# A bilinear feed-forward kernel behind memory attention: batch 0's output with plain weights, and all engines in the order of four written lists

## The chip, the cores and the metric

The kernel runs on one core of a Trainium2 chip. The metric is the device time of one launch in microseconds (us); less is better. The core has a matrix engine (TensorE; PE in the profile, its weight loads PEld), a vector engine (VectorE; DVE), a scalar engine (ScalarE; ACT), GpSimd (POOL) and a sync engine (SyncE; SP) that issues all of this kernel's DMAs. In this kernel each engine works through its own list of instructions and waits on semaphores for the others. TensorE's results land in PSUM banks, and ACT and DVE copy them out to the main on-chip memory, SBUF, where POOL's steps work too.

## The reference

There are 8 batches of 8 heads, 576 tokens, head size 64, and 32 memory slots:

```python
a   = softmax(phi, axis=slots)                      # tokens x 32
k_m = einsum('bhsm,bhsd->bhmd', a, k); v_m = einsum('bhsm,bhsd->bhmd', a, v)
x   = softmax(q @ k_m.T / 8) @ v_m                  # attention over 32 memories
out = ((x @ w1) * (x @ w2)) @ w3 @ w_out            # 512 -> 1024, 1024 -> 1024 -> 512
```

The weights arrive as 64-bit floats and the attention inputs as 32-bit floats.

## The kernel before

**The algebra.** The value memories are multiplied into w1 and w2 once per batch (the "M" steps, four per batch, line 316), so that per token only the attention weights over 32 memories per head remain to be multiplied: the "A" units (line 505), 16 per batch, make 128 rows of (x·w1) and (x·w2) for half a batch (288 tokens) each; ACT copies one of the two out of PSUM (`a_sb`, line 513) and DVE multiplies the other with it into `g` (line 515). W = w3·w_out is computed once, at the start, in sixteen product steps (W00 to W07 for its upper half of rows, W10 to W17 for the lower; line 411). The output of a batch is W's transpose times g.

**Precision.** Every product of the A and out units is made of three: an operand is split into a rounded high part (ACT) and the low rest (DVE or POOL), and high·high, low·high and high·low are summed in PSUM. So each operand that is used there costs an ACT step and a subtraction: `mh`/`ml` for M, `ah`/`al` for the attention weights, `sh`/`sl` for g (steps h and l, lines 541 and 547), `Wh`/`Wl` for W.

**Strassen.** The out product of a batch is a 2 x 2 block product (two halves of the tokens by two halves of the output rows) and is made with seven block products instead of eight, in the Winograd form: sums of g's blocks (POOL, lines 520 to 532) times sums of W's blocks. Each of the seven takes two "O" units of 12 matmuls (line 567), 14 per batch. Banks are named o, x and ab; `keep` copies intermediate results out (p1, u2, p5, p4), `result` adds and stores them (C11, C12, C21, C22; line 583). W's blocks need the same sums: `weights_of_out` (line 430) makes, with ACT, DVE and POOL, W0 (upper rows, with the right half replaced by a difference), W1 (lower rows as they are), W2 and W3 (further differences), each with a high and a low part. In the kernel before this is done during batch 0's A units, by the tokens K, T, V, D, E, F, G.

**Conversion.** Each of 22 weight blocks is loaded (line 362) and turned from 64 to 32 bits by `convert` (from line 364): a DVE step (line 390), two ACT steps (391, 393), two DVE steps (399, 400). Five load buffers are in flight; the last blocks are loaded into the attention's own tiles.

**Attention of a batch**, as a chain of named steps: top (DVE) exp (ACT) norm (DVE) turn0, turn4 (TensorE transposes, copied out by ACT) mem (TensorE, copied out by ACT) blocks (TensorE, copied out by DVE), then for each half n of the tokens sc (TensorE scores, transposed out by DVE) mx sb (DVE) ex (ACT) sm mu tr (DVE) ah (ACT) al (DVE).

**Order.** SP and TensorE follow the order in which the code emits. START (line 21) is the order up to the first A unit; in it ACT, DVE and POOL are ordered by the scheduler of the framework. From batch 0 on those three also follow the order of the code: FIRST (line 26) for batch 0's A units, with the last four conversions and the steps on W between them; BATCH_A (line 30) for the A units of the other batches; BATCH_O (line 31) for the out units of all batches. The next batch's attention (STREAM, line 35) is fitted in between by `ahead_slot` (line 597), which goes by a table of costs (line 40) and a limit of load, and which starts only at slot 13, that is, late in batch 0's A units. A tile's buffers are reused when all who read it are done.

Of the kernel before, what the change touches and what calls it, by code (L numbers as in the profile page):

```python
# [19 lines left out]

START = """
C C W00 C phi0 C top W01 C C C W02 kv0 C q0 W03 W04 exp norm C turn0 C W05 C W06 turn4 W07 C K1 mem K0 blocks W10
C W11 K3 K2 sc0 W12 C mx0 sb0 ex0 C sc1 mx1 sb1 ex1 C W13 W14 sm0 mu0 N C sm1 mu1 W15 C W16 W17 tr0 ah0 al0 N
tr1 ah1 al1
""".split()
# [13 lines left out]

COLUMNS = {"A": 439, "h": 0, "l": 727, "C11": 727, "C22": 727, "C21": 727, "C12": 727, "top": 1300, "norm": 330, "blocks": 1110,  # L40
           "sc": 876, "mx": 726, "sb": 726, "sm": 1100, "mu": 726, "tr": 726, "al": 726, "M": 1174, "N": 1174, "C1": 726,
           "C3": 1820, "D": 407, "E": 1060}
TENSOR = {"A": 1517, "O": 1517, "M": 910, "N": 910, "mem": 2300, "turn0": 770, "sc0": 500, "sc1": 500, "blocks": 200}
LIMIT = 2100


def groups(text):
    return [x.split() for x in text.split("|")]


def columns(what):
    return COLUMNS.get(what, COLUMNS.get(what.rstrip("0123456789"), 0))


@with_exitstack
def memory_attention__then__bilinear_ffn_kernel(
# [64 lines left out]
    def split(hi, lo, src):  # L121
        nc.scalar.copy(out=hi, in_=src)  # L122
        nc.vector.tensor_tensor(out=lo, in0=src, in1=hi.bitcast(F32), op=ALU.subtract)  # L123


# [36 lines left out]
    def attention(b):  # L162
# [22 lines left out]
        def turn(i, bank):  # L185
            ps = bank().rearrange("p k (c t x) -> p (k c) t x", c=2, t=NT)
            if i == 0:
                for c in range(4):
                    for t in range(NT):
                        at = t * D + c * P  # L190
                        nc.tensor.transpose(ps[:, c, t], v["ph"][:, t, at : at + P], ident)
                nc.scalar.copy(out=v["a"][:, :4], in_=ps)
            else:
                last = v["ph"].rearrange("p t s -> p (t s)")[:, 4 * P : 5 * P]
                nc.tensor.transpose(ps[:, 0, 0], last, ident)
                nc.scalar.copy(out=v["a"][:, 4, 0], in_=ps[:, 0, 0])

        def memories(bank):
            kvt = loaded.pop(("kv", b))
            v["kvm"] = att.tile([P, NT, 2 * D], F32, name="kvm")  # L200
            ps = bank()
# [10 lines left out]
            for h in range(4):  # L212
                for t in range(NT):
# [22 lines left out]
        def scores(n, bank):  # L236
# [6 lines left out]
            ps = [both[:, t, :HALF] for t in range(NT)]  # L243
# [9 lines left out]
            nb = NBLK // 2  # L253
# [479 lines left out]
```

## Time and profile before

| | |
|---|---|
| median of 3 runs | 568.89 us (568.81 to 569.41) |
| the profiled execution | 569.46 us, span 567.7 us |
| mean granted TensorE clock | 0.986 |
| busy share of the span: TensorE, DVE, ACT, POOL | 94%, 64%, 49%, 25% |
| DMA | 64.13 MB, 113 GB/s over the span |
| first matmul; first A unit | 9.07 us; 74.70 us |
| first A unit of batch 1, of batch 2 | 153.28 us; 216.46 us |
| last matmul begins | 562.30 us |

The profile is one execution, taken by the hardware profiler. A view of groups shows, for a line, engine and operation, how many instructions there were, their busy time, the mean of one in ns, and behind the bar the idle time of the engine just before them with the engine and line that ended it. A view of waits lists who waited for whom: us in total, times, longest. A timeline row has start, duration, engine, line, operation, and in square brackets the idle time before it. The times of matmuls overlap: their durations are modelled, and the distance between the starts of two is what one costs.

### The profile page before, as it was taken

The numbers are of one execution on the slowest core, as the hardware profiler recorded it, in microseconds if no ns is written. First come the engines' busy times: TensorE is split into PE (matmuls) and PEld (weight loads), VectorE is DVE, ScalarE is ACT, GpSimd is POOL, SyncE is SP. The second block draws the span as 40 slices with busy tenths as digits, with TensorE's granted clock in tenths as the row PEclk, the third lists the DMA queues.
The fourth block names the chain that finished last, engine by engine and source line by source line (L and its number), as shares of the span: only waits on it lengthen the run. The fifth ranks groups of instructions, "written<-read, shape, count | busy, mean of one in ns | idle before, by whom it ended". The sixth has DMA issues, their size and how long they took to land.

```text
span 567.7 us, 10851 instructions
## 1 busy us (share of the span) xinstructions
PE 532.0 (94%) x4504; PEld 448.6 (79%) x4504; DVE 365.9 (64%) x598; ACT 276.5 (49%) x465; POOL 141.2 (25%) x154
## 2 busy tenths in 40 slices
PE   3999996869889999999999999999999999999996
PEld 1454475757788899879988898889897998799996
DVE  4857957666744596548753885488448844695463
ACT  6867455564235443545254534453455435453351
POOL 0000016592011520233022502160207010611180
PEclk9999998979999999999999999999999999999999
DMA  8999530705410533043204311342114310001001
GB/s 321 408 382 388 199 97 21 249 0 190 147 42 2 170 105 104 2 169 105 69 36 168 105 64 43 119 133 84 43 51 149 116 64 2 1 26 60 1 22 63
DMA packets 28304, 64.13 MB, mean 113 GB/s; under 512 B 1632, under 2 KB 9824, under 8 KB 28256
## 3 DMA queue, kind: packets, MB, share of 16 engines
q1 hardware_dynamic: 28256, 63.45, 31.6%
q8 instruction: 35, 0.57, 0.4%
q14 instruction: 13, 0.11, 0.1%
HBM read 54.00 MB, written 9.44 MB: 112 GB/s over the span
## 4 chain that ended last, share of the span: by engine, by line
PE 78%; DVE 9%; ACT 7%; DMA 2%; POOL 1%; issue 1%; DVEq 0%; ACTq 0%
PE ab L505 29%; PE x L567 13%; PE o L567 11%; PE ab L567 4%; PE ab L411 4%; PE ab L316 4%; DVE ml L123 3%; ACT mh L122 3%; PE o L316 3%; PE o L411 3%; PE x L411 2%; PE x L205 2%; DVE mx L169 2%; ACT ph L175 2%; DMA raw<-in_w_out 1%
## 5 line engine op out<-in xcount | busy, mean ns | idle before, releaser
L505 PE MATMUL ab<-ah,mh 128*128 128x288 f32 x512 | 155.9, 305 | 8.4 <-DVE g L515 5.5
L505 PE MATMUL ab<-al,mh 128*128 128x288 f32 x512 | 152.7, 298 | 2.0 <-DVE al L292 2.0
L505 PE MATMUL ab<-ah,ml 128*128 128x288 f32 x512 | 151.6, 296 | 0.0
L515 DVE TENSOR_TENSOR g<-ab,a_sb 128x288 f32<-128x288 f32 x128 | 58.2, 455 | 112.0 <-ACT a_sb L513 112.0
L505 PEld LDWEIGHTS ab<-ah,mh 128*128 128x128 f32 x512 | 96.8, 189 | 26.2 <-DVE g L515 19.8
L513 ACT COPY a_sb<-ab 128x288 f32<-128x288 f32 x128 | 50.9, 398 | 124.1 <-PE ab L505 121.8
L547 DVE TENSOR_TENSOR sl<-g,sh 128x576 fp32r<-128x576 f32 x112 | 93.0, 842 | 16.2 <-ACT sh L541 16.1
L505 PEld LDWEIGHTS ab<-al,mh 128*128 128x128 f32 x512 | 96.9, 189 | 3.7 <-DVE al L292 3.7
L505 PEld LDWEIGHTS ab<-ah,ml 128*128 128x128 f32 x512 | 97.2, 190 | 0.0
L520 POOL TENSOR_TENSOR g<-g,g 128x288 f32<-128x288 f32 x32 | 30.7, 958 | 245.0 <-DVE g L515 245.0
L541 ACT CAST sh<-g 128x576 fp32r<-128x576 f32 x112 | 74.9, 675 | 33.8 <-PE x L567 11.9
L567 PE MATMUL o<-sh,Wh 128*128 128x288 f32 x192 | 58.4, 304 | 0.0
L567 PE MATMUL x<-sh,Wh 128*128 128x288 f32 x192 | 57.4, 299 | 0.0
L567 PE MATMUL o<-sh,Wl 128*128 128x288 f32 x192 | 57.2, 298 | 0.0
L567 PE MATMUL o<-sl,Wh 128*128 128x288 f32 x192 | 57.2, 298 | 0.0
L567 PE MATMUL x<-sh,Wl 128*128 128x288 f32 x192 | 56.6, 295 | 0.0
L567 PE MATMUL x<-sl,Wh 128*128 128x288 f32 x192 | 56.6, 295 | 0.0
L528 POOL TENSOR_TENSOR g<-g,g 128x288 f32<-128x288 f32 x32 | 26.0, 835 | 115.7 <-DVE sl L547 115.7
L567 PEld LDWEIGHTS x<-sh,Wh 128*128 128x128 f32 x192 | 36.2, 189 | 5.7 <-issue 5.7
L567 PEld LDWEIGHTS o<-sh,Wh 128*128 128x128 f32 x192 | 36.7, 191 | 3.3 <-issue 3.3
L411 PE MATMUL ab<-wo,w 128*128 128x512 f32 x64 | 29.7, 620 | 9.6 <-DVE wo L400 9.6
L567 PEld LDWEIGHTS o<-sh,Wl 128*128 128x128 f32 x192 | 36.7, 191 | 0.0
(125 smaller groups left out, 875.4 us busy)
## 6 DMA issues: line engine op xcount, KB each, us to landing
kv<-in_kv SPq DMA_DIRECT2D x16, 1024.0 KB, 7.3
q<-in_qT SPq DMA_DIRECT2D x8, 1152.0 KB, 5.5
outT<-c SPq DMA_DIRECT2D x32, 288.0 KB, 2.3
raw<-in_w3T SPq DMA_DIRECT2D x7, 1024.0 KB, 11.9
ph<-in_phiT SPq DMA_DIRECT2D x8, 576.0 KB, 3.9
raw<-in_w SPq DMA_DIRECT2D x4, 1024.0 KB, 17.6
raw<-in_w_out SPq DMA_DIRECT2D x3, 1024.0 KB, 10.0
kv<-in_w SPq DMA_DIRECT2D x3, 1024.0 KB, 14.4
```

The source lines that it names most:

```text
L122: nc.scalar.copy(out=hi, in_=src)
L123: nc.vector.tensor_tensor(out=lo, in0=src, in1=hi.bitcast(F32), op=ALU.subtract)
L316: nc.tensor.matmul(ps[g * M : (g + 1) * M, t], lhsT=vm[b % 2][d, g], rhs=w12_sb[q][d, :, g], start=True, stop=True,)
L411: nc.tensor.matmul(pw[r][i], lhsT=x[:, i * P : (i + 1) * P], rhs=wos[k // half][:, k % half], start=k == 0, stop=k == NF - 1,)
L505: nc.tensor.matmul(both[:, w, :HALF], lhsT=x[:, t, w, fc : fc + P], rhs=y[:, n, t * HALF : (t + 1) * HALF], start=i == 0, stop=i == len(to ...
L513: nc.scalar.copy(out=a_sb, in_=both[:, 0, :HALF])
L515: nc.vector.tensor_tensor(out=G[n, f // half][:, k], in0=both[:, 1, :HALF], in1=a_sb, op=ALU.mult)
L520: gp(out=low, in0=top, in1=low, op=ALU.subtract)
L528: gp(out=s2, in0=s2, in1=s3, op=ALU.subtract)
L541: nc.scalar.copy(out=hi, in_=src)
L547: nc.vector.tensor_tensor(out=lo, in0=src, in1=hi.bitcast(F32), op=ALU.subtract)
L567: nc.tensor.matmul(ps[:, j, :HALF], lhsT=x[s][:, 2 * part + k, jc], rhs=y[:, k], start=i in (1, 4, 2, 5) and part == 0 and k == 0 and t == ...
```

## The change

1. **Batch 0's out is made plainly**: four blocks of g against W's own blocks, 16 units "Q" (`plain_unit`) in place of 14 Strassen units, and four plain copies to the output (d0 to d3, `plain_result`). W's sums for Strassen are made in another order, and their high and low parts partly in batch 1's A units (tokens r, s, w, y, t, z), from copies in the `sh`/`sl` buffers (tokens a and b with a digit).
2. **Each step is on one engine.** Steps that held a TensorE part and a copy are cut in two (turn and turnc, mem and memc, block and blockc, sc and scc, M into M, Mh and Ml); an A unit becomes a generator of three steps (A: TensorE, a: ACT, g: DVE), a conversion one of five (C1 to C5); the sums on POOL become tokens of their own (f0 to f3, S1 to S4).
3. **The order of all engines, from the first instruction, is that of four lists**: START, FIRST (batch 0), SECOND (batch 1) and BATCH (batches 2 to 7). The table of costs, `ahead_slot` and `batches`' rules go. A token with "-" belongs to the batch's own attention, which is now finished inside its own A units; other attention tokens belong to the next batch. A token of an A unit or a conversion advances the next unit or conversion in turn by one step, whichever step that is.
4. `ah` and `al` have one buffer instead of two, and START holds one M step instead of two. Batch 1's A units run in the order (2 x 6 rows, then 2 x 2) instead of (2 x 4, 2 x 2, 2 x 2).

```diff
-START = """ C C W00 C phi0 C top W01 C C C W02 kv0 C q0 W03 W04 exp norm C turn0 ...
+START = """
+C1 C2 C2 C3 C3 C4 C5 C1 C2 C1 C4 C5 C3 C4 W00 phi0 C3 C4 C5 C2 C1 C1 C2 C5 W01 C4 q0 C3 C2 C3 C5 C4 C1 C5 C2 C3 C4 C1
+C3 C2 C1 W02 W03 C5 C4 kv0 top C5 C2 C4 exp norm C2 C1 C1 C3 C3 C5 W04 turn0 turnc0 C4 C5 W05 W06 C1 C4 turn4 C2 C3 C3
+C2 C5 C1 turnc4 W07 K1 Kt1 K0 C4 Kh1 Kt0 Kh0 K2 Kl1 mem K3 Kh3 Kl0 memc block Kh2 Kl3 C2 Kt2 C5 C1 C3 blockc C4 C5 W10
+Kl2 C2 C1 C3 C4 Kt3 sc0 C3 C5 sc1 C2 C1 W11 W12 scc0 C3 W13 C2 C4 mx0 C5 C1 sb0 C4 ex0 C1 sm0 scc1 W14 C5 C4 C2 C3 C2
+C1 M0 mx1 C3 C4 sb1 W15 W16 Mh0 C5 mu0 ex1 sm1 tr0 ah0 C5 Ml0 mu1 al0 tr1 W17 ah1 al1
+"""
 FIRST = """
+phi A a g A C1 M1 C2 C2 a g Mh1 Ml1 C3 C4 A A a g C1 a C5 g C4 C3 A A C5 a g C2 C1 a g M2 Mh2 C3 A a C4 Ml2 C1 g A C2
+a C5 C4 A a g D0 A C3 g C5 A a g q h0 l0 kv Dt0 a g E0 M3 Mh3 Ml3 D1 Et0 F0 D3 A a Dt1 g D2 E1 A A Dt2 a g Et1 F1 E2 A
+a g h1 l1 A a h3 g a g Et2 h2 l2 Dt3 Q E3 Q Q Et3 top h4 l3 Q l4 Q exp norm h5 Q l5 h6 turn0 l6 turn4 turnc4 Q turnc0
+mem memc Q h7 l7 d0 Q kv block F3 d1 Q F2 blockc M0 b1 a0 sc0 scc0 mx0 Mh0 sb0 ex0 Ml0 Q Q Q M1 a2 sc1 Q sm0 mu0 Mh1
+scc1 q a3 b0 tr0 ah0 Q Q d2 al0 a1 d3 Ml1
 """
+SECOND = """
+M2 Mh2 -mx1 r1 -sb1 A a -ex1 g r0 s0 A A a Ml2 r2 g -sm1 A w1 a g a -mu1 -tr1 g w3 -ah1 s1 w0 -al1 phi A a s2 y0 g A A
+r3 M3 a a s3 h1 g g y3 w2 y2 top A t0 y1 t1 a Mh3 t2 g z1 A z0 A f0 a a g g A f1 a Ml3 g exp A A a a g g f3 l1 norm
+turn0 h0 l0 f2 turnc0 t3 A a turn4 g h2 l2 turnc4 S2 A mem memc A z2 a g O a g h3 z3 h4 l3 S3 S1 l4 block O h5 O
+blockc M0 kv l5 S4 p1 h6 sc0 scc0 O Mh0 Ml0 p4 h7 l6 mx0 O O sb0 C11 M1 Mh1 l7 O h8 Ml1 ex0 l8 h9 h10 O sm0 l9 h11 u2
+l11 l10 O O sc1 p5 mu0 scc1 h12 tr0 h13 ah0 l13 l12 O O C22 q mx1 al0 sb1 O O C21 C12 ex1 sm1
+"""
+BATCH = """
+A A a g -mu1 -tr1 A M2 a g -ah1 a g -al1 Mh2 A a g h0 Ml2 a A a A a g g f1 a A a A phi g A M3 top f2 a g a g l0 f0 Mh3 h1
+a A a A Ml3 g A a g exp l1 f3 a g A turn0 a g A norm turnc0 a turn4 turnc4 A mem h2 memc a g g A block a l2 S2 g O
+blockc h3 l3 S3 kv h4 S1 l4 O M0 h5 Mh0 p1 O h6 l5 Ml0 S4 sc0 scc0 O h7 l6 O O p4 mx0 h8 M1 Mh1 l7 sb0 ex0 C11 h10 sc1
+l8 q scc1 O O h9 O h12 Ml1 u2 mx1 l9 sm0 l10 mu0 h11 l11 O O h13 l13 p5 l12 tr0 ah0 sb1 O C21 al0 O ex1 C22 O C12 sm1
 """
...
-                ready["A", b] = [att.tile([P, 2, S], F32R, name=x, tag=x, bufs=2) for x in ("ah", "al")]
+                ready["A", b] = [att.tile([P, 2, S], F32R, name=x, tag=x) for x in ("ah", "al")]
...
+        if step == "Kh":
+            high(0, i, raw)
+        if step == "Kl":
+            low(0, i, raw, gp)
+        if step == "Kt":
+            gp.tensor_tensor(out=t1, in0=two, in1=one, op=sub)
         if step == "D":
             high(1, i, pw[1][i])
+        if step == "Dt":
+            nc.vector.tensor_tensor(out=two, in0=pw[1][i][:, OH:], in1=t1, op=sub)
         if step == "E":
             low(1, i, pw[1][i], nc.vector)
+        if step == "Et":
+            nc.vector.tensor_tensor(out=raw4[0][:, i], in0=pw[1][i][:, :OH], in1=two, op=sub)
         if step == "F":
+            gp.tensor_tensor(out=one, in0=two, in1=one, op=sub)
+        if step == "r":
+            high(0, i, t1, upper)
+        if step == "s":
+            low(0, i, t1, gp, upper)
...
+    def plain_unit(m, G):
+        block, oh = m // 2, m % 2
+        n, part = block // 4, block % 4
+        if part == 0:
+            G["C", n, oh] = (pair_o, pair_x)[oh]() if n else pair_ab()
+        hi, lo, _ = G["X", block]
+        for j in range(2):
+            oc = slice(oh * OH + j * P, oh * OH + (j + 1) * P)
+            for k in range(2):
+                f = 2 * part + k
+                for t, (x, y) in enumerate(((Wh, hi), (Wl, hi), (Wh, lo))):
+                    nc.tensor.matmul(
+                        G["C", n, oh][:, j, :HALF],
+                        lhsT=x[f // half][:, f % half, oc],
...
+    def spare_bank(b, in_a):
+        if b == 0 and not in_a and n_o <= 8:
+            free.reverse()
+            return free[0]
+        return pair_x if in_a and b else pair_ab
...
-    with tile.TileContext(nc, schedule_with_timeline_sim=True) as tc, tc.manual_schedule(engines={mybir.EngineType.SP, mybir.EngineType.PE}):
+    with tile.TileContext(nc, schedule_with_timeline_sim=True) as tc, tc.manual_schedule(engines=ORDERED):
```

More of the change, by code (lines that the diff above doesn't have):

```diff
@@ L16 @@
 AX = mybir.AxisListType
+EngineType = mybir.EngineType
+ORDERED = {EngineType.SP, EngineType.PE, EngineType.Activation, EngineType.DVE, EngineType.Pool}
 START = """
[L22 to L25, printed above, removed]
-FIRST = """
-A C1 phi1 | A C2 C3 T0 | A C1 V0 | A C2 C3 T1 | A C1 V1 | A T2 C2 C3 | A N C1 V2 | A C2 C3 | A T3 V3 | A N kv1 q1 h0 |
@@ L37 @@
-al0 sm1 | mu1 | tr1 | ah1 | al1 phi
-"""
[L40 to L48, printed above, removed]
@@ L195, in turn, with turned @@
                 nc.tensor.transpose(ps[:, 0, 0], last, ident)
+            v["turned", i] = ps
+        def turned(i):
+            ps = v["turned", i]
+            if i == 0:
+                nc.scalar.copy(out=v["a"][:, :4], in_=ps)
+            else:
                 nc.scalar.copy(out=v["a"][:, 4, 0], in_=ps[:, 0, 0])
@@ L419, in memory_attention__then__bilinear_ffn_kernel, with move @@
     OH = DO // 2
-    raw0 = [att.tile([P, 2, S], F32, name="raw0", tag=x, bufs=2) for x in ("ah", "al")]
-    raw0 = [x[:, i, :DO] for x in raw0 for i in range(2)]
-    t4 = []
+    raw0 = const.tile([P, half, DO], F32, name="raw0", tag="Wl2")
+    raw1 = const.tile([P, half, OH], F32, name="raw1", tag="Wh3")
+    raw4 = []
+    moved = {}
+    def move(src):
+        n = src.shape[-1]
+        t = big.tile([P, 2, HALF], F32, name="moved", tag="sh" if n == DO else "sl", bufs=4)
+        t = t.rearrange("p a b -> p (a b)")[:, :DO] if n == DO else t[:, :, :n]
+        nc.scalar.copy(out=t, in_=src)
+        return t
@@ new lines, in weights_of_out @@
+        if step == "a":
+            moved["23", i] = move(raw)
+        if step == "b":
+            x = move(raw4[0][:, 2 * i : 2 * i + 2])
+            moved["4", 2 * i], moved["4", 2 * i + 1] = x[:, 0], x[:, 1]
+        if step == "r":
+            high(0, i, t1, upper)
+        if step == "s":
+            low(0, i, t1, gp, upper)
+        if step == "t":
+            high(3, i, moved["4", i], slice(0, OH))
+        if step == "z":
+            low(3, i, moved["4", i], gp, slice(0, OH))
+        if step == "w":
+            high(2, i, moved["23", i])
@@ new lines, in weights_of_out, with start @@
+        if step == "y":
+            low(2, i, moved["23", i], gp)
+    steps = {0: attention(0) | memory_weights(0)}
+    conversions = [convert(i) for i in range(len(tasks))]
+    at_stage = {f"C{i}": iter(conversions) for i in range(1, 6)}
+    def start(todo):
+        for what in todo:
+            key = what.rstrip("0123456789")
+            if what in at_stage:
+                next(next(at_stage[what]))
+            elif key == "W":
+                product(int(what[1]), int(what[2]))
+            elif key in ("K", "Kh", "Kl", "Kt"):
+                weights_of_out(key, int(what[-1]))
+            elif key in LOADS:
@@ L480, in start @@
                 load(what, 0)
             else:
-                in_x = what[:4] == "turn"
-                steps[0][what](pair_x if in_x else pair_o if what == "mem" else pair_ab)
-    last = len(START) - START[::-1].index("C")
+                steps[0][what]({"turn": pair_x, "mem": pair_o}.get(key, pair_ab))
+    todo = tokens(START)
+    last = len(todo) - todo[::-1].index("C5")
     with tc.tile_pool(name="init", bufs=1) as init:
@@ L681, in batches @@
-            assert next(ab, None) is None
-    ordered = {mybir.EngineType.Activation, mybir.EngineType.DVE, mybir.EngineType.Pool}
-    with tc.manual_schedule(engines=ordered):
-        batches()
+            ends = ((2, 4, 6, 8), (6, 8), (4, 6, 8))[min(b, 2)]
+            parts = [range(x, y) for x, y in zip((0, *ends), ends)]
+            units = [ab_unit(b, n, f, G) for fs in parts for n in range(2) for f in fs]
+            ab = {what: iter(units) for what in ("A", "a", "g")}
+            if b + 1 < B:
+                steps[b + 1] = attention(b + 1) | memory_weights(b + 1)
@@ L688 @@
+            assert next(ab["g"], None) is None
+    batches()
 _INS = ["qT", "kv", "phiT", "w1", "w2", "w3T", "w_out"]
```

293 lines of the change are left out of this document (122 added, 171 removed).

## The prediction

> **What bounds the kernel now.** I read the page, then TensorE's waits, then busy time in stretches that I cut where the chain of waits shows a stage to begin. Page: the span, TensorE's forty slices, its granted clock.
>
> ```profile
> span 567.7 us, 10851 instructions
> PE   3999996869889999999999999999999999999996
> PEclk9999998979999999999999999999999999999999
> ```
>
> TensorE is full from the thirteenth slice on. After the start it falls short, and its clock with it, only between about 85 and 165 us. Its waits say on whom:
>
> ```profile
> PE ab L411 <- DVE wo L400: 9.6, 2, 9.1
> PE ab L505 <- DVE g L515: 5.5, 5, 3.4
> PE ab L191 <- ACT ph L175: 5.2, 2, 4.9
> PE ab L505 <- DVE al L292: 2.0, 2, 1.6
> ```
>
> Of these the 9.1 us is the first weight block's way through DMA and conversion. The stretches are: that wait; the products W3·w_out (START, list of before); batch 0's A units; batch 0's out units; batch 1; batch 2 (batches 3 to 6 are like it); batch 7 with the tail. After the brackets stand TensorE's clock, the DMA share and GB/s.
>
> ```profile
> 0.00:9.07 9.07, 0.00 (x0) 0.00 (x1) 3.00 (x7) 4.90 (x7) 0.70 (x6) 1.00 0.76 266
> 9.07:74.70 65.63, 64.61 (x284) 28.12 (x284) 51.21 (x76) 43.76 (x48) 0.72 (x1) 1.00 0.88 333
> 74.70:112.40 37.70, 30.78 (x231) 26.45 (x224) 26.48 (x38) 23.91 (x39) 18.23 (x16) 0.95 0.40 134
> 112.40:153.15 40.75, 32.78 (x326) 28.55 (x324) 29.27 (x46) 19.56 (x35) 19.12 (x20) 0.92 0.31 110
> 153.15:216.46 63.31, 60.63 (x549) 54.43 (x550) 38.98 (x68) 27.43 (x51) 14.40 (x16) 0.97 0.25 84
> 216.46:275.60 59.14, 58.57 (x549) 52.61 (x549) 37.91 (x66) 27.35 (x50) 14.41 (x16) 1.00 0.27 91
> 512.14:567.70 55.56, 50.45 (x393) 48.01 (x391) 27.42 (x41) 20.19 (x37) 16.00 (x16) 0.98 0.09 30
> ```
>
> Columns after the length: PE, PEld, DVE, ACT, POOL. Batch 2 is TensorE's own work and nothing else: 58.57 of 59.14 us busy, DVE 64%, ACT 46%. Batch 0 has the same count of units, memory products and attention steps (30 units, 4 M, one attention) and takes 37.70 + 40.75 = 78.45 us, so it loses 78.45 - 59.14 = 19.3 us. Batch 1 loses 63.31 - 59.14 = 4.2. START is nearly dense. So 23.5 us can be won by order alone, all before 216 us; after that almost nothing.
>
> Where batch 0 loses them, in TensorE's order of time (the last two rows are the long stalls of the out units and of batch 1's start):
>
> ```profile
> 73.68 1.09 PE L316 MATMUL ab<-w,vm 64*32 64x512 f32 x16
> 77.20 0.40 PE L505 MATMUL ab<-ah,mh 128*128 128x288 f32 x1 [0.64 <-DVE ml L123]
> 89.33 0.40 PE L505 MATMUL ab<-ah,mh 128*128 128x288 f32 x1 [3.40 <-DVE g L515]
> 91.56 1.96 PE L316 MATMUL ab<-w,vm 64*32 64x512 f32 x16
> 119.22 0.47 PE L191 MATMUL ab<-ident,ph 128*128 128x128 f32 x1 [4.92 <-ACT ph L175]
> 153.28 0.40 PE L505 MATMUL ab<-ah,mh 128*128 128x288 f32 x1 [2.25 <-ACT ah L288]
> ```
>
> The M step behind the 3.40 us stall takes 1.96 us against 1.09: a long stall costs a second time, by the clock. The stall itself is made by the weights of out. In the stretch 75 to 122 us ACT waits for POOL, and DVE and POOL lengthen each other:
>
> ```profile
> ACT Wh L425 <- POOL raw L437: 6.8, 3, 3.7
> 84.40 2.10 DVE L400 CUSTOM_DVE_ANT_0 w<-w,ua 128x2048 uint16<-128x2048 uint16 x1
> 83.68 1.74 POOL L428 TENSOR_TENSOR Wl<-raw,Wh 128x512 fp32r<-128x512 f32 x1
> L400 DVE CUSTOM_DVE_ANT_0 w<-w,u 128x2048 uint16<-128x2048 uint16 x7 | 8.5, 1220 | 2.0 <-ACT u L393 1.8
> ```
>
> The copy a_sb stands on ACT behind the Wh that waits for POOL's step T; g stands behind a_sb, and the next A unit needs g's bank.
>
> **The change, part by part.** Terms from here on: one unit is 12 matmuls, and one product step is two of these pieces of the chain; then the helpers of a unit, of an M step, and of the softmax:
>
> ```profile
> 556.24 3.17 PE o L567 x24
> 43.38 1.72 PE x L411 x4
> L515 DVE TENSOR_TENSOR g<-ab,a_sb 128x288 f32<-128x288 f32 x128 | 58.2, 455 | 112.0 <-ACT a_sb L513 112.0
> L513 ACT COPY a_sb<-ab 128x288 f32<-128x288 f32 x128 | 50.9, 398 | 124.1 <-PE ab L505 121.8
> L123 DVE TENSOR_TENSOR ml<-ab,mh 128x1024 fp32r<-128x1024 f32 x18 | 22.0, 1224 | 20.5 <-ACT mh L122 20.4
> L122 ACT CAST mh<-ab 128x1024 fp32r<-128x1024 f32 x18 | 18.2, 1013 | 9.6 <-PE ab L316 8.9
> L169 DVE TENSOR_REDUCE mx<-ph 128x2 f32<-128x1152 f32 x8 | 10.7, 1342 | 0.0
> L175 ACT ACTIVATE ph<-ph,mx 128x576 f32<-128x576 f32 x16 | 12.3, 767 | 2.6 <-DVE mx L169 2.6
> L273 DVE TENSOR_REDUCE ss<-s_sb 128x18 f32<-128x576 f32 x16 | 11.8, 740 | 0.0
> L274 DVE TENSOR_SCALAR ss<-ss 128x18 f32<-128x18 f32 x16 | 2.8, 174 | 0.5
> L275 DVE RECIPROCAL ss<-ss 128x18 f32<-128x18 f32 x16 | 4.2, 262 | 0.5
> L279 DVE TENSOR_TENSOR s_sb<-s_sb,ss 128x576 f32<-128x576 f32 x16 | 12.0, 749 | 0.0
> L285 DVE STREAM_TRANSPOSE at<-s_sb 128x576 f32<-128x576 f32 x16 | 12.3, 769 | 0.0
> L288 ACT CAST ah<-at 128x576 fp32r<-128x576 f32 x16 | 10.7, 667 | 5.6 <-DVE at L285 5.6
> L292 DVE TENSOR_TENSOR al<-at,ah 128x576 fp32r<-128x576 f32 x16 | 12.0, 750 | 1.4 <-ACT ah L288 1.4
> 71.90 0.76 DVE L292 TENSOR_TENSOR al<-at,ah 128x576 fp32r<-128x576 f32 x1 [0.74 <-ACT ah L288]
> ```
>
> *Batch 0 without Strassen.* 16 units Q in place of 14 O: 2 × 3.17/2 = +3.2 us on TensorE, wholly on the path. It takes away batch 0's sums on POOL and 6 of 14 high/low splits. What it buys is that batch 0's out needs only W's own blocks: the differences (Kt, Dt, Et, F) no longer stand before any Wh that batch 0 uses, and r, s, w, y, t, z wait until batch 1's A units, where ACT is busy 27 of 63 us and POOL 14.
>
> *START.* TensorE's list is the sixteen product steps (16 × 2 × 1.72 = 55.0), one attention, and one M instead of two. The first product still waits for the same DMA, so 9.07 stays (the order of the first conversions may cost it half a microsecond, which the wait for the second pair absorbs). The end moves by the M that left: 74.70 - 1.1 = 73.6. q0's load now goes ahead of three weight loads on SP's queue; those are for the products of the second half, whose turn is ten and more us off, so nothing. New in START are eight POOL steps (Kt, Kl), and DVE is the tight engine there: 51.21 of 65.63 busy. al1 ended there at 71.90 + 0.76 = 72.66, so al0, a tr and an al earlier, at 71.1; the first A unit will want al0 at 73.6: 2.4 us of margin (al1 itself is wanted 4 us later). A collision costs 2.10 - 1.22 = 0.9 us by the rows; with none at one end and eight at the other, DVE ends 0 to 7 us later and the unit 0 to 4.7. I take three, since DVE spends but part of its time on instructions of that kind: 2.6 us, of which 0.2 gets past the margin.
> The Trainium skill (SBUF — State Buffer, Who interferes with whom) says that a DVE instruction with two SBUF inputs and a reading GpSimd instruction exclude each other and the later one blocks for the other's whole length. By that rule a collision is worth up to the POOL row's 1.74 us, and three of them would make this term 2.8 us, an estimate, in place of 0.2; the DVE row of this trace shows half of it, 0.9.
>
> *Batch 0's A units.* 16 units and three M: 25.4 + 3 × 1.2 = 29 us of TensorE. DVE had 26.5 us here; it gains a third ml (1.2) and loses POOL's interference, since POOL now has nothing here until F. So the 3.40 us stall and its cold clock go, and the ACT queue has no Wh that waits for POOL. Next late is the M step: it holds one of the two ab banks for 1.01 + 1.22 us and a hand-over of 0.1, while the unit between covers 1.59: 0.75 us, against the 0.64 measured at 77.20. Three times 0.75, and 0.4 for M2, whose last conversion ends behind two ACT steps: 2.6 us (0 if a conversion slips in elsewhere, 5 if DVE's order holds g back at two more places).
>
> *Batch 0's out units.* Attention of batch 1 begins after the third Q, its products take turns with Q, and memory and scores use the free o and x banks until C(0,·) is copied. The step that the 4.92 us went to, by the list: top and exp take 1.34 + 2 × 0.77 = 2.9 us, begin some 4 us after the first Q (behind the last g and the last two steps on W) and end at 7; turn0 stands behind the sixth Q, at 6 × 1.59 = 9.5. The later helpers have one Q or more each before the product that needs them. I keep 0.5. The second half of the softmax is left to batch 1.
>
> Sum for batch 0: a batch of before, 59.14, with one M more (1.1), two units more (3.2), and stalls 2.6 + 0.5 + 0.2: 66.7 us. It begins at 73.6 and ends at 140.3, where before stood 153.15.
>
> *Batch 1* carries r, s, w, y, t, z: twelve copies on ACT and twelve splits or so on POOL, all into idle time. I allow 0.5 (0 to 3, if one split is late for the third O): 59.14 + 0.5 = 59.6, so batch 2 begins at 199.9 instead of 216.46: 16.5 us earlier.
>
> *Batches 2 to 7.* TensorE's list is before's with other places for M and sc: the same number of changes of shape, so the same 59.14. A unit's bank comes free 1.59 + 0.3 + 0.40 + 0.46 = 2.8 us after its start and is needed at 3.2; no step that the list puts between fills the 0.4 twice in a row. al and ah have one buffer now; ah0 of the next batch is written in the out units, when all A units are done: nothing. Second softmax half: sum 0.74 + 0.17 + 0.26, mu 0.75, tr 0.77, ah 0.67, al 0.75, with g between, put al1 some 6.7 us after the batch begins, and the fifth A unit wants it at 7.4. I take 0 per batch, bounds -0.5 (the stalls left in batch 2, 59.14 - 58.57) and +0.5. The tail stays.
>
> Sum: 569.46 (profiled execution, span 567.7) - 16.5 = 553.0; it lies 0.57 over the median 568.89, so 552.4, rounded **552**.
>
> **Rivals.** *DVE and POOL lock each other out in START* for whole instructions: five of the eight at the POOL row's 1.74 are 8.7 us, less 2.4 of margin 6.3, so 558. It is the port rule above at work. For: 2.10 against 1.22. Against: the DVE row shows 0.9 for one. *The lists also clear the later batches*: 0.5 × 6 less, and no stall at M: 547.5. For: batch 2 has 0.57 of waits; against: it has no more. *The lists aren't executed as written*: conversions and A units are generators, and a token advances the next one by one step whatever its number says, so C2 may run a first stage. Worst, product steps and M wait for late conversions, 4 us: 556. Against: the order of each engine stays nearly the same, because steps only swap between neighbours. *Slower*: the second softmax half misses the fifth A unit in every batch. DVE's queue at a batch's end is C22, C12, the sum, then g, mu, tr, al; if C12's wait for the last O or a g in front holds it, TensorE waits for al1 seven times. The gain of 16.5 is used up at 16.5/7 = 2.4 us each, that is when al1 comes 3.1 us later than I have it; at 4 us, 7 × 3.3 = 23 us, 575. For: the wait for al L292 of 1.6 us stands in the profile; against: the 0.7 us margin and an idle third of DVE.
>
> **How the numbers follow.** Forecast 0.67, port lock 0.12, later batches cleared 0.10, list not as written 0.06, slower 0.05. From -0.5 per batch to the lock in START the cases span 546.5 to 559; that leaves out the slower rival and the ends of the forecast. This measurement can tell 0.2% (1.1 us) from nothing. Faster 0.94, same 0.01, slower 0.05.
>
> **What would show it.** Right: batch 2's first A unit at about 200 us; no TensorE wait over 1.5 us after 10 us; clock 1.00 in every slice from 85 to 165; waits of A units for ml of about 0.7, three times in batch 0; a period of 59.1. Wrong: a period over 60 with a wait for al; a first A unit after 76 us; POOL and DVE rows of 2 us between 39 and 55.

## The result: 543.36 us, and the profile after

The changed kernel takes 543.36 us in the median (541.85 to 544.74 over 4 runs) against 569.01 (568.81 to 569.41, four runs here) for the kernel before: a ratio of 0.9548, 95% interval 0.9512 to 0.9583, 25.6 us less. 552 was forecast, with 546.5 as the lowest end: right in sign, but a third of the gain was not foreseen. The executions lie on two levels, near 541.9 and near 544.7; the profiled one, 544.74 us with a span of 543.0, is of the upper level, and what lies between the two is found below. One execution of the kernel before (663.31 us) and one of the kernel with the two loads exchanged (990.6 us) ran at granted clocks of 0.751 and 0.899, in a slow state, and are left out of every range and ratio below. (The list BATCH as printed above has three tokens `a` too many in its first two lines; it holds sixteen. The list that ran reads "Ml2 A a A a g g f1 A a A phi g" and "Mh3 h1 A a A Ml3 g A a g" there.)

The page of the changed kernel, the same three lines as before:

```profile
span 543.0 us, 10835 instructions
PE   2998998999999999999999999999999999999997
PEclk9997999999999999999999999999999999999999
```

The dip between 85 and 165 us is gone from the clock, and from TensorE's slices but for one 8 at 81 to 95 us. A new one stands in the fourth slice of the clock, at 41 to 54 us. TensorE's waits (us in total, times, longest):

```profile
PE ab L435 <- DVE wo L424: 10.0, 2, 9.8
PE o L206 <- DMA kv<-in_kv: 2.0, 1, 2.0
PE ab L550 <- DVE ml L344: 1.8, 3, 0.6
PE ab L234 <- ACT kvm L227: 0.5, 1, 0.5
PE ab L328 <- DVE g L561: 0.2, 1, 0.2
```

Of the waits before, those for g (5.5), for the softmax (5.2) and for al (2.0) are gone, but for 0.2 for g. A wait for a DMA is new. Busy time by stretches, cut at the same events as before (first product, first A unit, first out unit, batch 1, batch 2, batch 3; then batch 7 with the tail):

```profile
0.00:9.78 9.78, 0.00 (x1) 0.00 (x1) 3.43 (x8) 5.50 (x8) 0.70 (x6) 1.00 0.77 271
9.78:78.38 68.60, 65.84 (x268) 29.55 (x268) 50.77 (x75) 45.40 (x51) 8.19 (x8) 0.95 0.83 313
78.38:110.85 32.47, 30.43 (x242) 26.30 (x241) 24.49 (x40) 21.40 (x33) 1.47 (x2) 1.00 0.48 160
110.85:143.43 32.58, 32.58 (x349) 29.49 (x347) 17.31 (x32) 14.97 (x26) 1.44 (x2) 1.00 0.39 126
143.43:200.91 57.48, 57.48 (x548) 52.23 (x548) 39.51 (x67) 32.23 (x65) 25.02 (x28) 1.00 0.22 76
200.91:258.47 57.56, 57.56 (x549) 51.99 (x548) 39.23 (x66) 27.82 (x51) 15.06 (x16) 1.00 0.34 113
488.75:543.00 54.25, 50.20 (x394) 47.96 (x392) 28.27 (x43) 20.29 (x37) 15.55 (x16) 0.99 0.10 34
```

Set beside the forecast of the profiled execution (553.0), stage by stage:

| stage | before | forecast | after | after less forecast |
|---|---|---|---|---|
| first A unit begins | 74.70 | 73.6 | 78.38 | +4.8 |
| batch 0 | 78.45 | 66.7 | 65.05 | -1.65 |
| batch 1 | 63.31 | 59.6 | 57.48 | -2.1 |
| batches 2 to 6, each | 59.14 | 59.14 | 57.57 | 5 × -1.57 = -7.85 |
| batch 7 and the tail | 55.56 | 55.56 | 54.25 | -1.3 |

These add up to -8.1, and 553.0 - 8.1 = 544.9 is the measured 544.74 but for rounding. (In the trace of the kernel before, the first A unit of batch 2 begins at 216.30 us, 0.16 ahead of the cut used above; batch 1 is shorter and the last row longer by that, and the period stays.) So two steps failed: the start lost 3.7 us where it should have won 1.1, 4.8 apart, and the later batches, taken as unchanged, gave 9.2. The experiments go after these two first, and then after what in batches 0 and 1 the two halves of the change are each worth.

### The profile page after: what moved, and what is told of

Read it like the earlier page. It is cut to its first block, busy times and chain, and to the rows that moved or that the text cites. A ratio compares the mean times of both kernels' runs of the same rounds, so it can differ in the third digit from the quotient of the medians.

```text
span 543.0 us, 10835 instructions
## 1 busy us (share of the span) xinstructions
PE 524.4 (97%) x4528; PEld 445.5 (82%) x4528; DVE 358.8 (66%) x588; ACT 276.9 (51%) x469; POOL 127.7 (24%) x142
## 4 chain that ended last, share of the span: by engine, by line
PE 89%; DMA 7%; ACT 2%; DVE 1%; SPq 1%; issue 0%
PE ab L550 37%; PE x L610 13%; PE o L610 13%; PE ab L610 4%; DMA kv<-in_kv 3%; PE ab L328 3%; PE x L435 3%; PE o L328 3%; PE o L435 3%; PE ab L631 2%; PE x L206 2%; DMA raw<-in_w_out 2%; PE ab L254 2%; PE x L631 1%; PE o L631 1%; DMA raw<-in_w3T 1%
## 5 line engine op out<-in xcount | busy, mean ns | idle before, releaser
L595 DVE TENSOR_TENSOR sl<-g,sh 128x576 fp32r<-128x576 f32 x106 | 86.6, 831 | 20.1 <-ACT sh L589 19.9
L566 POOL TENSOR_TENSOR g<-g,g 128x288 f32<-128x288 f32 x28 | 22.2, 807 | 155.0 <-DVE g L561 154.7
L574 POOL TENSOR_TENSOR g<-g,g 128x288 f32<-128x288 f32 x28 | 28.1, 1023 | 107.0 <-ACT a_sb L559 80.5
L610 PE MATMUL o<-sh,Wh 128*128 128x288 f32 x168 | 50.6, 301 | 0.0
L610 PE MATMUL x<-sh,Wh 128*128 128x288 f32 x168 | 50.5, 300 | 0.0
L610 PE MATMUL o<-sh,Wl 128*128 128x288 f32 x168 | 49.6, 295 | 0.0
L610 PE MATMUL x<-sh,Wl 128*128 128x288 f32 x168 | 49.6, 295 | 0.0
L610 PE MATMUL x<-sl,Wh 128*128 128x288 f32 x168 | 49.6, 295 | 0.0
L610 PE MATMUL o<-sl,Wh 128*128 128x288 f32 x168 | 49.5, 295 | 0.0
L610 PEld LDWEIGHTS o<-sh,Wh 128*128 128x128 f32 x168 | 31.6, 188 | 3.6 <-issue 3.6
L435 PEld LDWEIGHTS ab<-wo,w 128*128 128x128 f32 x64 | 12.5, 201 | 25.3 <-issue 14.3
```

What stands on the lines that cost most here:

```text
L435: nc.tensor.matmul(pw[r][i], lhsT=x[:, i * P : (i + 1) * P], rhs=wos[k // half][:, k % half], start=k == 0, stop=k == NF - 1,)
L566: nc.gpsimd.tensor_tensor(out=low, in0=top, in1=low, op=ALU.subtract)
L574: gp(out=s2, in0=s2, in1=s3, op=ALU.subtract)
L610: nc.tensor.matmul(ps[:, j, :HALF], lhsT=x[s][:, 2 * part + k, jc], rhs=y[:, k], start=i in (1, 4, 2, 5) and part == 0 and k == 0 and t == ...
```

## The experiments

### The start: where did 4.8 us go?

TensorE in the changed kernel, at the new dip of the clock:

```profile
40.40 0.64 PE L206 MATMUL o<-kv,a 128*32 128x128 f32 x16
43.09 2.36 PE L206 MATMUL o<-kv,a 128*32 128x128 f32 x48 [2.05 <-DMA kv<-in_kv]
46.59 0.73 PE L234 MATMUL ab<-ident,kvm 128*128 128x128 f32 x2 [0.53 <-ACT kvm L227]
47.12 3.53 PE L435 MATMUL x<-wo,w 128*128 128x512 f32 x4
```

and the transfer that it waits for, from the chain of waits:

```profile
24.31 18.74 DMA kv<-in_kv
```

The memory step stops after 16 of its 64 matmuls and waits 2.05 us for the second part of kv0, and the product step behind it takes 3.53 us where it takes 1.88 elsewhere. The list moved q0's load up and kv0's back: q0's load and one more weight load now lie ahead of kv0 on the queue, and SP issues it at 22.75 us where the kernel before issues it at 19.80.

**The two loads exchanged** (changed kernel, START only):

```diff
-... W01 C4 q0 C3 ... W02 W03 C5 C4 kv0 top ...
+... W01 C4 kv0 C3 ... W02 W03 C5 C4 q0 top ...
```

> The changed kernel with the places of kv0 and q0 in START exchanged, so that kv0's load stands ahead of three weight loads on SP's queue and q0's behind them. Theory A (the 2.05 us wait of mem for kv0, and the halved clock behind it, come from that order alone): no wait for kv0, clock 1.00 from 38 to 55 us, the first A unit near 74 instead of 78.4, the time about 540 in every run, and no spread of 541.9 to 544.7. Theory B (DMA is full there, 409 GB/s, so the wait only moves): TensorE waits 2 us or more for q0 at sc0 or for a weight block, and the time stays at 542 to 545.

Measured: 541.34 us (541.11 to 542.9 over five executions), ratio to the kernel before 0.9519 (0.9504 to 0.9534). The wait for kv0 and the half clock are gone, and the first A unit begins at 74.99. But this lies between the two theories: the time stays above 540, and a part of the loss moved to ACT. There a conversion step waited 3.80 us for a weight load, the steps behind it came late, and TensorE waits 1.21 us for the copy of the memories (kvm) instead of 0.53. The executions still lie on two levels (541.1 to 541.3 and 542.6 to 542.9); why was not followed further.

**The loads where the kernel before has them**, kv0 behind the twelfth weight fetch and q0 behind it:

```diff
-... W01 C4 q0 C3 C2 C3 C5 C4 C1 C5 C2 C3 C4 C1 C3 C2 C1 W02 W03 C5 C4 kv0 top ...
+... W01 C4 C3 C2 C3 C5 C4 C1 C5 C2 C3 C4 kv0 C1 C3 C2 C1 W02 W03 C5 C4 q0 top ...
```

> The changed kernel with the two attention loads put back where the kernel before issues them in relation to the weight loads: kv0 behind the twelfth weight fetch and q0 behind it, instead of q0 early and kv0 late. Theory A (the whole loss in START is the lateness of kv0 on the one queue, and the first exchange of the two tokens only moved part of it to the weight loads): neither kv0's wait nor the wait of the conversion steps for weight loads is left, the first A unit begins at 73.6 to 74.5 us instead of 78.38, and the time is 539.5 to 541. Theory B (START has its own new cost in the order of ACT and POOL, not in the loads): first A unit at 75 or later, as with the exchanged tokens, time 541.5 to 542.5.

Measured: 540.28 us (539.73 to 540.47), ratio 0.9488 (0.9475 to 0.9501), the fastest version of this study. Its TensorE:

```profile
41.19 1.95 PE L206 MATMUL o<-kv,a 128*32 128x128 f32 x64
44.05 0.59 PE L234 MATMUL ab<-ident,kvm 128*128 128x128 f32 x2 [0.53 <-ACT kvm L227]
74.08 0.70 PE L550 MATMUL ab<-ah,mh 128*128 128x288 f32 x1
```

All 64 matmuls of the memory step now run in one piece, and the first A unit begins at 74.08. Theory A holds: the loss in START was the place of the loads, kv0's above all. It also removes the two levels of the executions: these four runs lie within 0.74 us. Of the 4.3 us won back (78.38 to 74.08) some 2.9 are the clock's: three other versions with the START of the changed kernel kept the full clock in their traces (the experiments with turn0, M0 and M2 below), and their first A unit begins at 75.27 to 75.63.

**memc ahead of the copy K3 on ACT**, on top of that, for the 0.53 us that are left at L234:

```diff
-... mem K3 Kh3 Kl0 memc block ...
+... mem memc K3 Kh3 Kl0 block ...
```

> The kernel with the loads as before, and memc ahead of the copy K3 and the rounding Kh3 on ACT. Theory A (ACT's list makes memc, and so the block products, stand behind work on W that nobody waits for): the wait of the block products for kvm, 0.5 to 1.2 us in the traces of the changed kernel, goes, and the time is 0.5 to 1 us below the kernel with only the loads moved. Theory B (the wait is filled or moves to the next product step): less than 0.3 us between the two.

Measured: 540.44 us (539.63 to 540.77), ratio 0.949 (0.9477 to 0.9503): no different. The row at L234 has the same 0.53. Theory A falls, and ACT's row in the kernel with only the loads moved shows why:

```profile
43.63 0.62 ACT L227 ACTIVATE kvm<-o,sm 128x128 f32<-128x128 f32 x2 [0.32 <-PE o L215]
```

ACT had no step on W in hand; it was itself waiting for the memory step. The 0.53 us are the copy and its hand-over.

### The later batches: where do 1.57 us per batch come from?

By kind of work, from one first A unit to the next, the changed kernel spends less in the A units (26.18 us instead of 26.65), in the transposes of the softmax, turn0 with turn4 (0.82 instead of 1.52), in the scores (1.30 instead of 1.51) and in the out units (22.90 instead of 23.11). These are sums of distances between starts in the two traces. In the kernel before, turn0 in one of the later batches, and the fifth A unit of the same batch:

```profile
340.97 0.29 PE L505 MATMUL ab<-ah,mh 128*128 128x288 f32 x1
341.24 0.40 PE L505 MATMUL ab<-al,mh 128*128 128x288 f32 x1
341.48 0.30 PE L505 MATMUL ab<-ah,ml 128*128 128x288 f32 x1
341.62 0.29 PE L505 MATMUL ab<-ah,mh 128*128 128x288 f32 x1
...
356.28 0.29 PE L505 MATMUL ab<-ah,ml 128*128 128x288 f32 x1
356.55 0.33 PE L191 MATMUL x<-ident,ph 128*128 128x128 f32 x1
357.31 0.98 PE L191 MATMUL x<-ident,ph 128*128 128x128 f32 x7 [0.43 <-ACT ph L175]
```

and VectorE of the kernel before, at the first of these:

```profile
340.44 0.75 DVE L292 TENSOR_TENSOR al<-at,ah 128x576 fp32r<-128x576 f32 x1
```

Undisturbed matmuls of a unit start 0.13 us apart, but each is drawn with 0.29 us. So the starts 340.97, 341.24, 341.48 lie 0.27 and 0.24 apart, 0.25 us of waiting in all, and no bracket shows it: the drawn rows overlap or touch. al1 ends at 341.19, and the matmul that reads al starts at 341.24. The fifth A unit of each later batch waited for al1. In turn0 0.14 is hidden in the same way at 356.55, and only 0.43 stands in a bracket. Five experiments undo or make these, one by one and together.

**The gap alone, in the kernel before**: one empty place in the stream between the softmax and its transposes.

```diff
-top | exp | norm turn0 | turn4 | mem | ...
+top | exp | | norm turn0 | turn4 | mem | ...
```

> The kernel before, with one empty place in STREAM between exp and turn0. Theory A (in before's later batches turn0 stands directly behind exp and TensorE waits for it, which the busy shares hide): turn0 takes 0.8 instead of 1.5 us, the period goes from 59.14 to about 58.4, and the time falls by about 6 x 0.7 = 4 us to 565. Theory B (batches 2 to 7 were TensorE's own work, and the list's gain there is in something else, such as fewer changes of shape): the period stays 59.1 and the time within 1 us of 569.

Measured: 559.44 us (557.5 to 561.79), ratio 0.9832 (0.9811 to 0.9852). The period falls from 59.14 to 58.30, so 0.84 per batch, about 5 us over the six later batches. The rest comes earlier: batch 0's stall for the softmax falls from 4.92 to 1.69 us, and batch 1 begins at 149.46 instead of 153.28. One empty place in a list is worth 9.6 us, more than a third of what the whole change is worth.

**turn0 one A unit earlier, in the changed kernel**:

```diff
-... exp l1 f3 a g A turn0 a g A norm ...
+... exp l1 f3 a g turn0 A a g A norm ...
```

> The changed kernel with turn0 one A unit earlier in BATCH, directly behind exp as in the kernel before. Theory A (the distance of turn0 from exp is worth 0.7 us of the 1.57 that each later batch won): the period rises from 57.57 to about 58.3, the time by 6 x 0.7 = 4 us. Theory B (the gain per batch lies in the rest of the order): no change beyond 1 us.

Measured: 544.67 us (544.36 to 547.57), ratio 0.9578 (0.9558 to 0.9598). The profiled execution, at a clock of 0.999, is to be set beside the 541.9 level: +2.8 us. The period rises to 58.14. Its waits have the old line back:

```profile
PE x L187 <- ACT ph L171: 1.6, 5, 0.3
```

**M0 and sc0 directly behind the first O, as before**:

```diff
-blockc h3 l3 S3 kv h4 S1 l4 O M0 h5 Mh0 p1 O h6 l5 Ml0 S4 sc0 scc0 O ...
+blockc M0 sc0 h3 l3 S3 kv h4 S1 l4 O h5 Mh0 p1 O h6 l5 Ml0 S4 scc0 O ...
```

> The changed kernel with M0 and sc0 put back directly behind the first O of the out units in the list for batches 2 to 7, as in the kernel before; all else as changed. Theory A (of the 1.57 us that each later batch became shorter, 0.7 come from turn0's place and the rest from M and the scores standing later, when their banks and operands are ready): the period goes from 57.57 to 57.9 to 58.2, the time rises by 2 to 3.5 us. Theory B (places of M and scores cost nothing, the rest comes from elsewhere): period within 0.1 of 57.57, time within 0.7 us.

Measured: 544.01 us (543.94 to 544.24), ratio 0.9556 (0.9543 to 0.9569), 2.1 us over the 541.9 level; period 58.03. Theory A holds, with the time at its lower end: +0.46 per batch. The new line in its waits says what for, the copy of an out bank, which the scores need free:

```profile
PE ab L254 <- DVE c L657: 2.1, 5, 0.4
```

**M2 behind the fifth A unit, as before**:

```diff
-A A a g -mu1 -tr1 A M2 a g -ah1 a g -al1 Mh2 A a g h0 Ml2 A a A a g g f1 A a A ...
+A A a g -mu1 -tr1 A a g -ah1 a g -al1 A a g h0 A M2 a Mh2 A a g g f1 Ml2 A a A ...
```

> The changed kernel with M2 and its two steps moved two A units later in the list for batches 2 to 7, behind the fifth A unit as in the kernel before; al1 stays where it is in the order of VectorE. Theory A (in the kernel before the fifth A unit of every batch waited about 0.25 us for al1, hidden in drawn matmul ends, and the change removed that wait by putting an M step of 1.02 us ahead of the fifth unit): the wait comes back, period 57.57 + 0.25 = 57.8, the time rises by 1.5 to 1.8 us over the 541.9 of the undisturbed executions. Theory B (the place of M2 is of no account): period within 0.1 of 57.57, time unchanged.

Measured: 543.5 us (543.15 to 546.24), ratio 0.956 (0.9538 to 0.9583), 1.6 over the 541.9 level; period 57.81. The fifth A unit of this kernel shows the pattern of the kernel before again:

```profile
320.13 0.29 PE L550 MATMUL ab<-ah,mh 128*128 128x288 f32 x1
320.40 0.40 PE L550 MATMUL ab<-al,mh 128*128 128x288 f32 x1
320.64 0.29 PE L550 MATMUL ab<-ah,ml 128*128 128x288 f32 x1
```

0.27 and 0.24 us between starts, to the hundredth. So al1's lateness was there before, and the change hid it behind an M step of 1.02 us set ahead of the fifth unit, without making al1 earlier.

**All three places as before**, the last three edits together:

```diff
-... A M2 a g ... exp l1 f3 a g A turn0 a g ... O M0 h5 Mh0 ... S4 sc0 scc0 O ...
+... A M2 a Mh2 ... exp l1 f3 a g turn0 A a g ... blockc M0 sc0 h3 ... S4 scc0 O ...
```

> The changed kernel with three places of its list for batches 2 to 7 put back as in the kernel before: turn0 one A unit earlier, M0 and sc0 directly behind the first O, M2 behind the fifth A unit. Theory A (these three places are the whole gain of the later batches, and they add): period 57.57 + 0.57 + 0.46 + 0.25 = 58.85, against 59.14 before; the time rises by 7 to 9 us over 541.9. Theory B (they overlap, since each is a wait that another can cover, or something else carries a good part): period under 58.5.

Measured: 551.33 us (548.42 to 551.5), ratio 0.9676 (0.9653 to 0.9699); the one execution without the clock drop is the 548.42, 6.5 us over the 541.9 level, where 7 to 9 was expected. Batch 2 in the profiled execution:

```profile
200.87:259.73 58.86, 58.13 (x550) 52.40 (x548) 38.45 (x66) 27.54 (x51) 15.00 (x16) 1.00 0.33 111
```

58.86, where 57.57 + 0.57 + 0.46 + 0.25 = 58.85 was expected. The three add, and account for 1.28 of the 1.57 us. The gap in the kernel before was worth 0.84 where turn0's return cost 0.57, and the difference of 0.27 is nearly the rest. Half of it can be read from the traces: the gap shortens the transposes by 0.70 (1.52 to 0.82) and the A units by 0.14 (26.65 to 26.51), which is the hidden wait in front of 356.55, while the return lengthens the transposes alone. The time fits too: turn0, M0 and sc0 are steps for the next batch and act in the five batches 2 to 6, M2 in six, and 5 × (0.57 + 0.46) + 6 × 0.25 = 6.65 stands against the 6.5 measured; the 7 to 9 expected was too much for these counts.

### Batches 0 and 1: plain blocks or the order?

**Only the plain units, in the old machinery**: the kernel before with batch 0's out made plainly and W's sums moved to batch 1, still with its groups, costs and load limit.

```diff
-A C1 phi1 | A C2 C3 T0 | A C1 V0 | A C2 C3 T1 | ... | A F3 G2 G3 h3 l2
+A C1 phi1 | A C2 C3 | A C1 | A C2 C3 | ... | A F3 h3 l2
+Q l3 | Q h4 | Q | Q h5 l4 | ... | Q d1 l7 | Q a0 b0 | Q | Q a1 b1 | ...
+A r0 s0 w0 | A r1 s1 y0 | A r2 s2 w1 | ... | A y2 w3 | A y3 | A h0 t0 | ...
```

> The kernel before with batch 0's out made plainly and the sums of W moved as in the change, but in the old machinery of order (START by the scheduler, ahead_slot from slot 13, the old lists from batch 2 on). Theory A (what batch 0 won is the weights' steps leaving its A units: no ACT wait for POOL, no 3.4 us stall): batch 0's A units lose 4 us instead of 10, two units cost 3.2, the rest stays: about 566. Theory B (what it won is the new order, above all the earlier attention of batch 1): the 4.9 us wait for exp stays, two units more, 569 to 573.

Measured: 566.75 us (565.1 to 566.9), ratio 0.995 (0.9938 to 0.9961). Batch 0's A units, its out units, batch 1, and a later batch:

```profile
75.11:107.31 32.20, 29.65 (x233) 26.04 (x225) 24.10 (x40) 21.23 (x32) 2.67 (x3) 1.00 0.44 156
107.31:146.66 39.35, 35.61 (x347) 31.06 (x348) 18.76 (x34) 16.05 (x29) 0.74 (x1) 0.96 0.30 106
146.66:211.06 64.40, 58.97 (x549) 52.17 (x547) 39.23 (x66) 33.06 (x65) 25.21 (x28) 1.00 0.26 88
274.01:333.08 59.07, 58.49 (x550) 52.51 (x548) 37.88 (x66) 27.34 (x50) 14.39 (x16) 1.00 0.27 91
```

The A units take 32.20 us instead of 37.70, as in the changed kernel (32.47): that part of the gain belongs to the plain blocks and the moved sums, by whatever order. But the out units take 39.35, little less than the 40.75 before and far from the 32.58 of the changed kernel, and most of what batch 0 won is lost again: batch 1 takes 1.1 us more than before and batch 2 3.8 more (62.95, from 211.06 to 274.01). The wait for ah of 2.25 us that stood at batch 1's first A unit (153.28) now stands at batch 2's (2.24 at 211.06).

**Plain units and the gap together**, in the old machinery, with this edit on top of the last:

```diff
-top | exp | norm turn0 | turn4 | mem | ...
+top | exp | | norm turn0 | turn4 | mem | ...
```

> The kernel before's machinery with plain units in batch 0 and the sums on W moved (as in the run of that part alone, 566.75), and in addition one empty place between exp and turn0 in the stream of attention steps. Theory A (the two gains are separate: 5.6 us in batch 0's A units by the plain units, and 0.8 per batch plus the 4.9 us stall by the gap): 566.75 - 5 (six batches of 0.84) - 1 to 4 (the exp stall in batches 0 and 1, of which 2.1 us are left there) = 557 to 561. Theory B (both feed on the same slack of DVE and ACT in batch 0): no better than the gap alone, 559.4 or above.

Measured: 558.27 us (557.43 to 559.26), ratio 0.9806 (0.9792 to 0.9821). Theory A by its range, but set beside the gap alone (0.9832) the plain blocks add only 0.26%, some 1.5 us: 0.5% and 1.7% apart give 1.9% together. Its waits show what neither touches:

```profile
PE o L624 <- DVE ml L130: 2.4, 1, 2.4
PE ab L537 <- DVE al L299: 2.3, 4, 1.6
PE ab L537 <- ACT ah L295: 2.2, 1, 2.2
```

The waits for ml, al and ah, 6.9 us, I read as an attention and an M step that the load limit lets in too late; no run tried that by itself. In the changed kernel, where they have places of their own in the lists, only three waits of 0.6 for ml are left. Of the 29.3 us that the best version gains on the kernel before in its own comparison (569.57 to 540.28), 11 are to be had without the lists, and some 18 come with them. No run has the lists without the plain blocks, so what the blocks are worth under the new order stays open.

**An earlier start for batch 1's attention, in the kernel before**:

```diff
-    first_slot = 13
+    first_slot = 9
```

> The kernel before with the attention of batch 1 allowed from slot 9 of batch 0's A units instead of slot 13, and nothing else changed. Theory A (batch 0's out units lose their time because the attention starts late, so that turn0 waits 4.92 us for the softmax and the clock falls): the stall and the cold clock behind it go, 5 to 8 us less, time about 562. Theory B (VectorE is full in batch 0's A units with the conversions and the weights of out, so that the maximum of the softmax, 1.34 us each, delays g and so the A units): gain under 2 us, or a loss.

Measured: 569.38 us (568.65 to 570.67), ratio 1.0007 (0.9998 to 1.0016). This says nothing on either theory: the order of instructions on every engine is the same as in the kernel before, so the number is not what holds the stream back. Whether an earlier attention alone would have removed batch 0's stall stays open.

## Why the prediction was right or wrong, step by step

**Wrong: "Batches 2 to 7 ... the same number of changes of shape, so the same 59.14", with -0.5 as the bound from "58.57 of 59.14 us busy".** This is the step that took the result out of the range. Busy time of TensorE was read as work, but matmuls drawn with 0.29 us and started 0.13 us apart cover a wait of up to 0.16 at each place. The 0.57 us that I saw idle were turn0's bracket for the most part (0.43); 1.57 were to be had. They were turn0 standing directly behind its softmax (0.57 when put back), the scores and M0 standing before an out bank was free (0.46), and al1 late for the fifth A unit (0.25); the remaining 0.28 is only in part assigned above. The rival that the lists clear the later batches (chance 0.10) had the direction and was sized from the same 0.57. The Trainium skill (Perfetto Trace Analysis, Tensor Engine Instruction) says that the profiler estimates a matmul's end from its size, so that its time is a model and not a measurement; the rows above show what follows from that, starts 0.27 apart beside a drawn 0.29. The right measure was there: distances between starts, summed by kind, against the 0.13 of the same row's neighbours.

**Wrong: "q0's load now goes ahead of three weight loads ... so nothing".** I followed q0 and not kv0, which the same line of the list moves back past the other loads, and so missed that the memory step needs it at 40 us. The term put at nothing is a wait of 2.05 us and a clock at half after it: 4.3 of the 4.8 us, by the run with the loads restored. The sign of being wrong that I had named, a first A unit after 76 us, came true, but through the load, not through DVE and POOL.

**Right, START otherwise**: with the loads restored, the first A unit begins at 74.08, against 73.6. The first product began 0.6 later than before there (9.69 against 9.07), as allowed for, though it was not absorbed.

**Right that it costs next to nothing, wrong in size: DVE and POOL in START.** The forecast took three collisions, 2.6 us. In the changed kernel there are hardly any, since DVE stood idle for the transposes behind kv0 while POOL worked:

```profile
47.36 0.28 DVE L241 TENSOR_SCALAR km<-ab 64x128 f32<-64x128 f32 x1 [8.33 <-PE ab L234]
...
48.41 0.79 DVE L422 TENSOR_SCALAR w<-w 128x1024 int32<-128x1024 int32 x1
49.62 1.26 DVE L424 CUSTOM_DVE_ANT_0 w<-w,u 128x2048 uint16<-128x2048 uint16 x1 [0.41 <-ACT u L416]
```

With the loads restored they do collide, and six of DVE's rows beside POOL's grow by 4.6 us in all (the last section has four of them); yet al0 ends at 72.70, 1.6 us later than the 71.1 worked out without a collision and 1.4 us ahead of the first A unit, so they cost nothing. The rival of 558 is refuted with the collisions present.

**Right, batch 0's A units**: the stall of 3.40 us is gone, and what is late next is the M step, three times, in these sizes:

```profile
85.58 0.40 PE L550 MATMUL ab<-ah,mh 128*128 128x288 f32 x1 [0.54 <-DVE ml L344]
94.35 0.40 PE L550 MATMUL ab<-ah,mh 128*128 128x288 f32 x1 [0.63 <-DVE ml L344]
104.41 0.40 PE L550 MATMUL ab<-ah,mh 128*128 128x288 f32 x1 [0.61 <-DVE ml L344]
```

1.8 us and 0.2 for g, where 2.6 was forecast. **Right, its out units**: the softmax ends at 117.18 and turn0 runs at 120.37, 9.5 us after the first Q, without a wait; 16 Q and the attention make 32.58 us, all of it busy. Of the 1.65 us by which batch 0 beat the forecast, 0.6 are M's stalls and 0.5 the helpers' term; that the rest is the hidden waits in 59.14, the base of that sum, is argued and not tested.

**Right, batch 1's borrowed work costs nothing** (57.48, less than a later batch), and **right, al1 ends 6.57 us after the batch begins** (6.7 forecast), so the slower rival never came near. But I did not look at how the kernel before stood there: its al1 was as late (6.61), and its fifth unit was already waiting. Of the rival that the lists aren't executed as written there is no sign: after the first product, TensorE waits 0.2 us in all for conversions.

**Luck**: batch 2 begins at 200.91, and "at about 200" stood among the signs of being right. Two errors cancel there: the start is 4.8 us late, and batches 0 and 1 are 3.8 short of their forecast.

## What to carry to other kernels

Measure a steady state of TensorE by distances between starts, kind by kind, and compare each distance with the best one of the same shape in the same trace; here a busy share of 99% hid 1.0 of the 1.57 us per batch that a new order removed. When an order is rewritten, follow every load that changes its place in a shared queue to the first instruction that needs all of its parts. And before a large rewrite of an order, try the smallest edits that its profile suggests: one empty place in a list was worth 9.6 of the 25.6 us.

## What the runs showed of the hardware

**The clock fell after every wait of 2.05 us or more, after one of 1.69, and not after one of 1.93.** This counts TensorE's waits behind the first product in all traces. Fourteen of them last 2.05 us or longer, and after each the granted clock is 0.50 for about 3.4 us or twice that (0.95 in the mean of 68.60 us in the changed kernel's START is 6.9 us at one half). With a wait of 1.93 us for kv0 (M2 behind the fifth unit) the clock stays, and the product step behind it takes 1.88 us; with 2.05 (the changed kernel) and 2.12 (all three places) that step takes 3.53 and 3.62:

```profile
43.17 1.52 PE L206 MATMUL o<-kv,a 128*32 128x128 f32 x48 [1.93 <-DMA kv<-in_kv]
...
46.02 1.88 PE L435 MATMUL x<-wo,w 128*128 128x512 f32 x4
```

But the length alone does not decide. In the kernel before with the empty place, a shorter wait is followed by a clock of 0.50 (third number from the end of the lower row):

```profile
116.09 0.33 PE L191 MATMUL ab<-ident,ph 128*128 128x128 f32 x1 [1.69 <-ACT ph L175]
117.00:119.50 2.50, 2.50 (x12) 2.50 (x13) 2.50 (x4) 2.50 (x6) 2.50 (x2) 0.50 0.00 0
```

What decides between such waits was not tested. From the end of kv0's wait to the start of the second product step it is 4.6 us with the full clock (43.17 to 47.73) and 7.4 in the changed kernel (43.09 to 50.48): 2.8 us more, which is the distance between its two levels, 541.9 and 544.7. The Trainium skill (TensorE: Matmul & The Clock Gate, What's actually happening) states that the clock is halved after an idle window of about 3.4 us, which runs freely. The waits of 1.69, 2.05 and 2.12 us are shorter than the window and were still followed by a halving, so here a wait of half the window's length could already be followed by half the clock; the half clock itself, about 3.4 us or twice that, agrees with the window.

**An execution that is late at the first products loses less at kv0.** In the five traced executions with the changed kernel's START, kv0's wait ends at 42.8 to 43.2 us; what differs is when TensorE reaches the memory step. Some of the very first matmuls start 0.85 us apart and the later ones 0.43. With two to four such distances the memory step begins at 40.2 to 40.6 us and waits 1.93 to 2.12; with five or six it begins at 41.4 to 41.5, waits 1.00 and 0.68, and the clock stays. So one and the same START meets the clock drop in some executions and not in others.

**DVE instructions with one input are lengthened by POOL too.** In the kernel with the loads restored, DVE between 40 and 51 us, while POOL is busy without a break:

```profile
42.19 2.29 DVE L424 CUSTOM_DVE_ANT_0 w<-w,uw 128x2048 uint16<-128x2048 uint16 x1
...
45.84 1.58 DVE L422 TENSOR_SCALAR w<-w 128x1024 int32<-128x1024 int32 x1
47.55 1.53 DVE L424 CUSTOM_DVE_ANT_0 w<-w,u 128x2048 uint16<-128x2048 uint16 x1
49.01 1.83 DVE L412 TENSOR_SCALAR uw<-raw 128x1024 uint16<-128x1024 uint16 x1
```

The same instructions take 1.21, 0.67, 1.21 and 0.74 without POOL beside them (52.49, 64.19, 65.46 and 51.86 in the same trace). The rows of lines 412 and 422 have one input, those of line 424 two. Each loses 0.3 to 1.1 us, and the forecast, which went by the two-input step alone, had too few rows that could.
